# Attention products on GpSimd, and a seventh block in three passes for 12 more experts

## The chip, the cores and the metric

The kernel runs on one core of one Trainium2 chip. The core has five engines with a queue of instructions each: TensorE (PE in the profile, with its weight loads as PEld), VectorE (DVE), ScalarE (ACT), GpSimd (POOL) and SyncE (SP), which issues most of the DMAs. The engines run side by side and wait for each other through semaphores; each works through its own queue strictly in order. The metric is the device time of one execution in microseconds (us), lower being better.

## The reference

A block of sketched polynomial attention feeds a mixture of four experts. Cut to what is computed:

```python
# q, k, v: (4 batches, 4 heads, 1088 positions, 32); S1, S2: (8, 32)
def phi(x):
    a = einsum('rd,bhsd->bhsr', S1, x)
    b = einsum('rd,bhsd->bhsr', S2, x)
    return einsum('bhsi,bhsj->bhsij', a, b).reshape(..., 64)   # 64 products of factors
q_p, k_p = phi(q), phi(k)
kv = einsum('bhsf,bhsd->bhfd', k_p, v);  z = k_p.sum(axis=2)
x = (q_p @ kv) / (q_p @ z + 1e-6)          # -> (4352 tokens, 128)
p = domain_probs / (domain_probs.sum(-1) + 1e-9)
for e in range(4):                         # w1: (128, 1024), w2: (1024, 128) each
    out += p[:, e:e+1] * (maximum(x @ w1[e], 0) @ w2[e])
```

Everything is float32. The products in `phi` are what the change moves: for the keys 64 products per head and position (the "key products"), and the same for the queries (the "factor products").

## The kernel before

**Tiling.** The 4352 tokens are cut into 11 chunks (`CHUNKS`: 128, 448, 512, seven of 448, 128). A chunk goes through the four experts one after the other. An expert's 1024 hidden units are 8 blocks of 128, and a *half step* is one block of one expert for one chunk; a full chunk has 32 half steps and a step has two. `first` (from L1123) makes a block's hidden values: three matmuls of the kind fp32r, L1174, L1175 and (half a step later, in `third`) L1226, on weights and tokens that were split into parts called a, b and d. Between the second and the third ScalarE rescales the sum in PSUM (L1176). The first and the last chunk, of 128 tokens, go another way (`plain`), and so do the first two experts of chunk 1 (`whole`: three passes in the first matmul, plain fp32 in the second, L1276).

**The second matmul** of a block adds into the output, and there are two ways for it. In six of an expert's eight blocks (`THREE`) it is three fp32r matmuls (L1295, with `ha`, `hb`, `hd` as moving data): ScalarE makes `ha` (L1230), VectorE makes `hb` (L1202), and for two blocks at once `hd` (L1205). In the other two blocks ScalarE only takes the maximum with zero into `hid` (L1235) and the second matmul is one fp32 matmul, which the trace shows as two records. `MORE_IN` names the pairs (chunk, expert) in which seven blocks go through three passes and one stays fp32; `more_weight_parts` splits the weights of that seventh block (two activations on ScalarE, two operations on VectorE) at the steps in `MORE_AT`. `DEAL` and `DEAL_MORE` say how many half steps after a block's first matmul each of its second matmuls stands in TensorE's queue; the order is written out by hand and doesn't depend on when data is ready.

**After an expert**, `gather` (L1318) weights its output with the gate: ScalarE and VectorE bring the two PSUM banks together in `ev` (L1298, L1327), and GpSimd multiplies with the gate and adds to the chunk's `total` (L1334, L1336; two or four instructions). `ev` and `total` have one buffer each, `gate` has two, and SP's queue reloads a gate (L385) after GpSimd has read the one before it.

**Attention** is cut into three units per batch (`UNITS`), and its work is laid between the half steps by a plan (`lay_plan`): a list of pieces with a cost in VectorE time, each with an earliest place, so many half steps after another piece. `piece` takes the next piece when the credit that every half step brings suffices. For each unit: `qturn` (transposes on VectorE), `visit` of the unit before it (which projects this unit's queries on TensorE, copies them, L787, writes them to DRAM, L789, and reads them back spread over 128 partitions into `qp` and `qb`, L796 and L798), two `product` pieces (L810, at least `LAND` = 6 half steps after that visit), the unit's own `visit` on TensorE (`attend_products`: the factor products times the summed keys), `inverse`, `scale` and `out`. `out` transposes the unit's tokens and sends them over DRAM into `ring` (SP: four writes `xd<-y`, L744, then one read `ring<-xd`, L753), from where ScalarE and VectorE split them for the first matmul (`token_parts`, L925 and L928) at a fixed step, eight half steps ahead of their chunk. For each batch the keys go through `turn`, `project`, `sum` and four `products` pieces (L472, 576 elements per partition each); the sums over the keys (`key_sums`, 72 matmul records) stand in the visit of the last unit of the batch before, for batch 1 in a piece of its own.

What a visit's place is can be counted in TensorE's queue. Before, the projections of the visits stand behind the first matmul of half steps number 4, 15, 47, 65, 93, 107, 126, 157, 172 and 199, counted from the beginning of chunk 1, and the sums of the keys behind 38, 93 and 157.

Of the kernel before, what the change touches and what calls it, by code (L numbers as in the profile page):

```python
# [12 lines left out]
ALU = mybir.AluOpType  # L13
# [11 lines left out]
def kernel(  # L25
# [62 lines left out]
        ("b", 1, 1, 16), ("d", 1, 1, 17), ("b", 2, 0, 16), ("d", 2, 0, 17), ("b", 2, 1, 17), ("d", 2, 1, 18),  # L88
        ("a", 3, 1, 17), ("b", 3, 0, 19), ("b", 3, 1, 19), ("d", 3, 0, 20), ("d", 3, 1, 20),
    ]  # L90
    W2_AT = (36, 38), (41, 43), (45, 47), (65, 67)
    TOKENS_AT = 11, 12

    CHUNKS = [P, 448, 512] + [448] * 7 + [P]
    NC = len(CHUNKS)
    MORE_IN = {(7, 0), (7, 2), (8, 0), (8, 1), (8, 2), (9, 0), (9, 1), (9, 2), (9, 3)}
    MORE_AT = {0: (100, 102), 1: (113, 115), 2: (116, 118), 3: (129, 131)}
    START = [sum(CHUNKS[:m]) for m in range(NC)]
    assert all(sum(u) == S for u in UNITS) and sum(CHUNKS) == B * S

# [367 lines left out]
    def key_product(b, t0, n, p, x, eng, kf=None):  # L468

        if b:  # L470
            fs = lambda k, dims: _ap(fss[b], 0, P, 32 * (NT * p + t0) + R2 * x + k, [[32, n]] + dims)
            eng.tensor_tensor(  # L472
                out=_ap(kps[b], 0, P, 256 * t0 + P * p + R * x, [[256, n], [R2, R], [1, R]]),
                in0=fs(0, [[1, R], [0, R]]), in1=fs(R, [[0, R], [1, R]]), op=ALU.mult,
            )
            return
        src, off = (kf, P * p) if kf is not None else (fss[b], 32 * (NT * p + t0))
        eng.tensor_tensor(  # L478
            out=_ap(kps[b], 0, P, 256 * t0 + P * p + 64 * x, [[256, n], [32, 2], [R, 4], [1, R]]),
            in0=_ap(src, 0, P, off + 4 * x, [[32, n], [R2, 2], [1, 4], [0, R]]),  # L480
            in1=_ap(fss[b], 0, P, 32 * (NT * p + t0) + R, [[32, n], [R2, 2], [0, 4], [1, R]]),
            op=ALU.mult,
        )
# [44 lines left out]
    def key_pieces(b):  # L528

        for r in range(3):  # L530
            add(0.69 if r < 2 else 0.23, lambda r=r: key_turn(b, r), f"turn{r}")
        values, kf = value_copy(b), {}

        def project(gi):
            kf[gi] = held(psum(ps_h, "h"))
            key_project_wide(b, gi, kf[gi])

        def summed(gi):
            key_add(b, gi, kf[gi])
            free()  # L540
            next(values, None)
            if gi == 2 and 1 < b < B - 1:
                load_batch(b + 1)

        for gi in range(3):
            add(0.1, lambda gi=gi: project(gi), f"project{gi}", (f"turn{gi}", 2))
            add(0.2 if gi == 2 else 0.42, lambda gi=gi: summed(gi), f"sum{gi}", (f"project{gi}", 1))
        for p in range(2):
            for x in range(2):
                add(0.76, lambda p=p, x=x: key_product(b, 0, NT, p, x, nc.vector), "products")  # L550

    sums = {}

# [5 lines left out]
    def key_end(b):  # L559

        def blocked():
            key_blocks(b, sums.pop(b))
            free()

        if b == 1:
            add(0.1, lambda: key_sums(b), "keysum", ("products", 3))
        add(0.29, blocked, "keyblocks", ("keysum" if b == 1 else "visit", 1))

    def unit_parts(b, c, n):
# [237 lines left out]
    def unit_product(w, p):  # L807

        n, (qp, qb) = later[w][2], factors[w]
        nc.vector.tensor_tensor(out=qp[p][:, 0:n], in0=qp[p][:, 0:n], in1=qb[p][:, 0:n], op=ALU.mult)  # L810

    def unit_visit(w):

# [15 lines left out]
    def add(cost, run, name, after=None):  # L829

        plan.append((cost, run, name, after))

    def lay_plan():

        of_first = queries(0, P, UNITS[0][1])
        costs = [0.62] * 9 + [0.05] * 4 + [0.4, 0.55, 0.6, 0.1, 0.1]
        distances = {12: ("first8", 3), 13: ("first12", 1), 16: ("first15", 2), 17: ("first16", 2)}
        for at, cost in enumerate(costs):
            add(cost, lambda: next(of_first, None), f"first{at}", distances.get(at))
        covers.append((len(plan), P + UNITS[0][1]))  # L840
        add(vector_us(later[0][2]), lambda: unit_turn(0), "qturn", ("start", 2 * NQ - 2))
        add(0.1, lambda: unit_project(0), "visit", ("qturn", 6))
        add(0, lambda: None, "wait", ("start", 2 * NQ + 2))
        keys = {}
        for b in range(1, B):
            now_on, plan[:] = list(plan), []
            key_pieces(b)
            keys[b], plan[:] = list(plan), now_on
        for w, (b, c, n, u) in enumerate(later):
            if b == 0:  # L850
                plan.extend(keys[1][:9])
            else:
                at = {(1, 0): (1, 9, 13), (1, 1): (2, 0, 3), (1, 2): (2, 3, 5), (2, 1): (3, 0, 3), (2, 2): (3, 3, 9)}
                if (b, u) in at:
                    k, z0, z1 = at[b, u]
                    plan.extend(keys[k][z0:z1])
                if b == 1 and u == 0:
                    key_end(b)
            more = w + 1 < len(later)
            if more:  # L860
                add(vector_us(later[w + 1][2]), lambda w=w: unit_turn(w + 1), "qturn")
            for p in range(2):
                add(vector_us(n), lambda w=w, p=p: unit_product(w, p), "product", ("visit", LAND if w else LAND + 1))

            last = 0 < b < B - 1 and u == len(UNITS[b]) - 1
            if last:
                plan.extend(keys[b + 1][(5, 9)[b - 1] :])

            def visit(w=w, more=more, then=b + 1 if last else None):
                if then:  # L870
                    key_sums(then)
                if more:
                    unit_project(w + 1)
                unit_visit(w)

            add(0.1, visit, "visit", ("products" if last else "product", 3))
            if last:
                key_end(b + 1)
            add(0.4, lambda w=w: inverse.__setitem__(w, attend_inverse(*products[w])), "inverse", ("visit", 1))
            add(vector_us(n), lambda w=w: over.__setitem__(w, attend_scale(*products[w], inverse.pop(w))), "scale")  # L880
            add(vector_us(n), lambda w=w: unit_out(w), "out")
            covers.append((len(plan), S * b + c + n))
# [560 lines left out]
    def to_due(i):  # L1443

        m, kq = steps[i]
        e, f = divmod(kq, NP)
        if plain(m):
            due.append((2 * i + 5, 2 * i, 0, i, None, None))
        elif whole(m, e):
            late = (0, 0, 0, 0, 1, 1, 1, 1)[2 * f : 2 * f + 2] if e else (0, 0)  # L1450
            due.extend((2 * i + 3 + j + late[j], 2 * i, j, i, j, None) for j in range(2))
        elif f == 0:
            for at, (p, slot) in enumerate(deal_of(m, e).items()):
                k = int(p[1])
                due.append((2 * i + slot, 2 * i, at, i + k // 2, k % 2, p[0]))
        due.sort(key=lambda d: d[:3])
# [93 lines left out]
```

## Time and profile before

| what | value |
|---|---|
| time, median of 3 runs (lowest to highest) | 448.81 us (448.4 to 449.26) |
| the profiled execution: its time, its span | 448.88 us, 447.1 us |
| busy: PE, PEld, DVE | 442.2 us (99%), 370.7 us (83%), 371.4 us (83%) |
| busy: ACT, POOL | 333.8 us (75%), 128.4 us (29%) |
| granted clock of TensorE | 1.000 |
| DMA | 38.47 MB, mean 86 GB/s |
| DVE: L472 key products, 12 x 0.789 us | 9.5 us |
| DVE: L810 factor products, 20, by size 0.351 to 0.708 us | 11.8 us |
| POOL: L1334 and L1336, 126 instructions | 104.8 us |

The span is the time from the first to the last instruction of the profiled execution; the 1.8 us between it and the time lie around it. The busy time of PE counts the matmuls from the start of one to its modelled end, and one begins before the one before it has ended, so the distance from one start to the next is what a matmul costs when TensorE is the limit. The chain of waits goes back from the last instruction to whatever released each step. A line such as `L1176 ACT ... | 155.5, 540 | 74.9 <-PE h L1175 69.2` gives the busy time, the mean in ns of one, and the idle time of the engine before it with what ended it.

### The profile page before, as it was taken

What the parts mean: (1) busy time and instruction counts of PE and PEld (TensorE: products, weight loads), DVE (VectorE), ACT (ScalarE), POOL (GpSimd) and SP (SyncE); (2) the same over time, 40 slices, a digit from 0 to 9 for tenths busy, and PEclk for the clock granted to TensorE, in tenths of its full rate; (3) what the DMA queues carried; (4) which work ended last, traced back from release to release, by engine and by line L of the source; (5) the groups of instructions that cost most, each with busy time, mean ns of one, the idle gap of its engine ahead of it and who ended that gap; (6) DMA issues with size and microseconds to landing.
All of it is one profiled execution on the core that took longest, in us unless ns stands there. A gap on an engine that the chain in (4) does not pass through costs nothing.

```text
span 447.1 us, 8728 instructions
## 1 busy us (share of the span) xinstructions
PE 442.2 (99%) x3030; PEld 370.7 (83%) x3030; DVE 371.4 (83%) x634; ACT 333.8 (75%) x710; POOL 128.4 (29%) x211
## 2 busy tenths in 40 slices
PE   8999999999999999999999999999999999999997
PEld 5887678777788888888888888888888888888887
DVE  5998689897988896888879869898899898898853
ACT  4478878677867876778688767788788888888831
POOL 7346123211323141212321312124223313331430
PEclk9999999999999999999999999999999999999999
DMA  6956264014323402252242142410230021016401
GB/s 194 314 135 173 66 180 95 26 44 115 94 62 86 120 23 81 52 128 71 77 113 28 22 125 66 115 55 21 76 70 22 27 61 40 21 39 216 157 1 30
DMA packets 53620, 38.47 MB, mean 86 GB/s; under 512 B 26920, under 2 KB 49640, under 8 KB 53576
## 3 DMA queue, kind: packets, MB, share of 16 engines
q1 hardware_dynamic: 52776, 37.31, 31.2%
q0 software_dynamic: 576, 0.53, 0.6%
q8 instruction: 24, 0.39, 0.4%
q14 instruction: 20, 0.16, 0.1%
q10 hardware_dynamic: 224, 0.07, 0.1%
HBM read 32.68 MB, written 5.21 MB: 85 GB/s over the span
## 4 chain that ended last, share of the span: by engine, by line
PE 95%; DVE 2%; DMA 1%; issue 0%; SPq 0%; ACT 0%; DVEq 0%; ACTq 0%
PE o L1295 40%; PE h L1226 14%; PE h L1174 13%; PE h L1175 13%; PE h L261 7%; PE o L1276 3%; PE o L261 3%; PE h L456 1%; DMA kn<-in_k_dram 1%; DVE qp L609 1%; DMA vn<-in_v_dram 0%; DVE qa L900 0%; DVE rd L641 0%; DVE kp L478 0%; DVE qf L889 0%
## 5 line engine op out<-in xcount | busy, mean ns | idle before, releaser
L1176 ACT ACTIVATE h<-h 128x448 f32<-128x448 f32 (+1 forms) x288 | 155.5, 540 | 74.9 <-PE h L1175 69.2
L1202 DVE SCALAR_TENSOR_TENSOR hb<-h,ha 128x448 fp32r<-128x448 f32 (+1 forms) x213 | 130.3, 622 | 40.4 <-ACT ha L1230 37.7
L1205 DVE SCALAR_TENSOR_TENSOR hd<-ha,hb 128x896 fp32r<-128x896 f32 (+2 forms) x111 | 123.9, 1116 | 10.7 <-PE o L1295 1.9
L1174 PE MATMUL h<-xa,wa 128*128 128x448 f32 (+1 forms) x288 | 131.5, 457 | 0.0
L1230 ACT ACTIVATE ha<-h 128x448 fp32r<-128x448 f32 (+1 forms) x213 | 116.6, 547 | 0.0
L1334 POOL TENSOR_TENSOR ev<-ev,gate 128x256 f32<-128x256 f32 (+1 forms) x54 | 47.6, 881 | 214.5 <-DVE ev L1327 203.6
L1226 PE MATMUL h<-xd,wd 128*128 128x448 f32 (+1 forms) x288 | 107.3, 373 | 0.1
L1175 PE MATMUL h<-xb,wb 128*128 128x448 f32 (+1 forms) x288 | 105.8, 368 | 0.0
L1295 PE MATMUL o<-ha,vab 128*128 128x448 f32 (+1 forms) x204 | 76.4, 374 | 0.0
L1174 PEld LDWEIGHTS h<-xa,wa 128*128 128x128 f32 x288 | 54.2, 188 | 18.4 <-issue 13.5
L1175 PEld LDWEIGHTS h<-xb,wb 128*128 128x128 f32 x288 | 54.2, 188 | 17.8 <-issue 13.7
L1226 PEld LDWEIGHTS h<-xd,wd 128*128 128x128 f32 x288 | 54.0, 188 | 9.2 <-ACT h L1176 2.3
L1295 PE MATMUL o<-hd,vd 128*128 128x448 f32 (+1 forms) x204 | 60.1, 369 | 0.0
L1295 PE MATMUL o<-hid,w_sb 128*128 128x448 f32 (+1 forms) x118 | 54.7, 545 | 0.0
L1295 PE MATMUL o<-hb,vb 128*128 128x448 f32 (+1 forms) x136 | 50.1, 368 | 0.0
L1336 POOL TENSOR_TENSOR total<-total,ev 128x256 f32<-128x256 f32 (+1 forms) x54 | 45.0, 832 | 4.2
L1235 ACT ACTIVATE hid<-h 128x448 f32<-128x448 f32 (+1 forms) x75 | 41.5, 553 | 0.9 <-PE h L1226 0.8
L1295 PEld LDWEIGHTS o<-ha,vab 128*128 128x128 f32 x204 | 38.3, 188 | 4.2 <-issue 0.2
L1295 PEld LDWEIGHTS o<-hd,vd 128*128 128x128 f32 x204 | 38.1, 188 | 3.6
L1334 POOL TENSOR_TENSOR total<-ev,gate 128x256 f32<-128x256 f32 (+1 forms) x18 | 12.2, 699 | 71.7 <-issue 54.1
L1295 PEld LDWEIGHTS o<-hb,vb 128*128 128x128 f32 x136 | 25.5, 188 | 2.1
L1295 PE MATMUL o<-hb,vab 128*128 128x448 f32 (+1 forms) x68 | 25.3, 372 | 0.0
(151 smaller groups left out, 455.1 us busy)
## 6 DMA issues: line engine op xcount, KB each, us to landing
gate<-gates SPq DMA_DIRECT2D x22, 224.0 KB
kn<-in_k_dram SPq DMA_DIRECT2D x4, 544.0 KB
vn<-in_v_dram SPq DMA_DIRECT2D x16, 128.0 KB
w_last<-in_moe_w_dram SPq DMA_DIRECT2D x4, 512.0 KB
w_sb<-in_moe_w_dram SPq DMA_DIRECT2D x3, 512.0 KB
w_sb<-in_moe_w_dram SPq DMA_DIRECT2D x6, 256.0 KB
qp<-qd SPq DMA_DIRECT2D x6, 224.0 KB
qb<-qd SPq DMA_DIRECT2D x6, 224.0 KB
```

What stands on the lines that cost most here:

```text
L261: nc.tensor.matmul(out(s), weights(s), moving(s), **flags)
L1174: nc.tensor.matmul(g, wa[:, e, w], xa, start=True, stop=False)
L1175: nc.tensor.matmul(g, wb[:, e, w], xb, start=False, stop=True)
L1176: nc.scalar.activation(g, g, ACTF.Copy, scale=1.0 + R12)
L1202: nc.vector.scalar_tensor_tensor(out=hb, in0=g, scalar=0.0, in1=high, op0=ALU.max, op1=ALU.subtract)
L1205: nc.vector.scalar_tensor_tensor(out=d2, in0=a2.bitcast(F32), scalar=R12, in1=b2.bitcast(F32), op0=ALU.mult, op1=ALU.subtract)
L1226: nc.tensor.matmul(g, w, x, start=False, stop=True, skip_group_check=True)
L1230: nc.scalar.activation(ha, g, ACTF.Relu, scale=NEAR)
L1235: nc.scalar.activation(hid[i][j], g, ACTF.Relu)
L1295: nc.tensor.matmul(acc[m, e][o][:, 0:n], w, h, start=first_one, stop=last)
L1334: nc.gpsimd.tensor_tensor(out=to[:, x], in0=ev[:, x], in1=g[:, x], op=ALU.mult)
L1336: nc.gpsimd.tensor_tensor(out=total[m][:, x], in0=total[m][:, x], in1=ev[:, x], op=ALU.add)
```

## The change

Three things change together.

- The key products of `key_pieces` (L472) and the factor products of the later units (L810) are issued on GpSimd rather than on VectorE. In the plan their costs become smaller (0.4 and 0.3), they are kept apart from each other (two half steps between key products, one between factor products), and a visit comes at least 4 half steps after the second factor product, or 5 after the fourth key product, where it was 3.
- `MORE_IN` grows from 9 to 21 pairs: (1,2), (2,1), (3,0), (3,2), (4,0), (4,1), (5,0), (5,2), (6,0), (6,1), (7,1) and (8,3) are new. In each, one block's second matmul becomes three fp32r matmuls instead of one in fp32. The seventh block's weights, which were split in chunks 6 to 8, are split in chunks 1, 2 and 4 (`MORE_AT`).
- Two small moves in chunk 1: one piece of the weight splits comes half a step later (`W2_AT`), and one second matmul of its second expert half a step earlier (`late`).

```diff
-    W2_AT = (36, 38), (41, 43), (45, 47), (65, 67)
+    W2_AT = (36, 38), (41, 43), (45, 48), (65, 67)
...
-    MORE_IN = {(7, 0), (7, 2), (8, 0), (8, 1), (8, 2), (9, 0), (9, 1), (9, 2), (9, 3)}
-    MORE_AT = {0: (100, 102), 1: (113, 115), 2: (116, 118), 3: (129, 131)}
+    MORE_IN = {(1, 2), (2, 1), (3, 0), (3, 2), (4, 0), (4, 1), (5, 0), (5, 2), (6, 0), (6, 1), (7, 0), (7, 1), (7, 2)}
+    MORE_IN |= {(m, e) for m in (8, 9) for e in range(E)}
+    MORE_AT = {0: (37, 39), 1: (35, 36), 2: (22, 24), 3: (68, 70)}
...
-                add(0.76, lambda p=p, x=x: key_product(b, 0, NT, p, x, nc.vector), "products")
+                add(
+                    0.4,
+                    lambda p=p, x=x: key_product(b, 0, NT, p, x, nc.gpsimd),
+                    "products",
+                    ("products", 2) if p or x else ("sum2", 1),
+                )
...
-            add(0.1, lambda: key_sums(b), "keysum", ("products", 3))
+            add(0.1, lambda: key_sums(b), "keysum", ("products", 5))
...
-        nc.vector.tensor_tensor(out=qp[p][:, 0:n], in0=qp[p][:, 0:n], in1=qb[p][:, 0:n], op=ALU.mult)
+        nc.gpsimd.tensor_tensor(out=qp[p][:, 0:n], in0=qp[p][:, 0:n], in1=qb[p][:, 0:n], op=ALU.mult)
...
-                add(vector_us(n), lambda w=w, p=p: unit_product(w, p), "product", ("visit", LAND if w else LAND + 1))
+                add(
+                    0.3,
+                    lambda w=w, p=p: unit_product(w, p),
+                    "product",
+                    ("product", 1) if p else ("visit", LAND if w else LAND + 1),
+                )
...
-            add(0.1, visit, "visit", ("products" if last else "product", 3))
+            add(0.1, visit, "visit", ("products" if last else "product", 5 if last else 4))
...
-            late = (0, 0, 0, 0, 1, 1, 1, 1)[2 * f : 2 * f + 2] if e else (0, 0)
+            late = (0, 0, 0, 0, 0, 1, 1, 1)[2 * f : 2 * f + 2] if e else (0, 0)
```

After the change the projections stand behind half steps 4, 16, 47, 67, 97, 111, 132, 161, 175 and 200, and the sums of the keys behind 35, 97 and 161.

## Prediction

> **What bounds the kernel now.** I read the busy shares first, then the chain of waits, then the list of who waited for whom, and last TensorE's and SP's instructions in order of time. The page:
>
> ```profile
> PE 442.2 (99%) x3030; PEld 370.7 (83%) x3030; DVE 371.4 (83%) x634; ACT 333.8 (75%) x710; POOL 128.4 (29%) x211
> ...
> PE 95%; DVE 2%; DMA 1%; issue 0%; SPq 0%; ACT 0%; DVEq 0%; ACTq 0%
> ...
> L1205 DVE SCALAR_TENSOR_TENSOR hd<-ha,hb 128x896 fp32r<-128x896 f32 (+2 forms) x111 | 123.9, 1116 | 10.7 <-PE o L1295 1.9
> L1334 POOL TENSOR_TENSOR ev<-ev,gate 128x256 f32<-128x256 f32 (+1 forms) x54 | 47.6, 881 | 214.5 <-DVE ev L1327 203.6
> ```
>
> TensorE is the bound: 95% of the chain are matmuls. In the list of waits TensorE (PE, PEld) appears after the start only with small entries, the largest with a cause being the third pass behind ScalarE's rescaling, 2.3 us in all, 7 times. So work taken from VectorE gains nothing by itself; what counts is what TensorE executes, and whether something begins to be late for it. TensorE in order of time, in chunk 6:
>
> ```profile
> 288.16 0.36 PE L1174 MATMUL h<-xa,wa 128*128 128x448 f32 x1
> 288.36 0.37 PE L1175 MATMUL h<-xb,wb 128*128 128x448 f32 x1
> 288.56 0.36 PE L1226 MATMUL h<-xd,wd 128*128 128x448 f32 x1
> 288.76 0.56 PE L1295 MATMUL o<-hd,vd 128*128 128x448 f32 x2
> 289.17 0.91 PE L1295 MATMUL o<-hid,w_sb 128*128 128x448 f32 x2
> 289.57 0.71 PE L1174 MATMUL h<-xa,wa 128*128 128x448 f32 x1
> 290.12 0.36 PE L1175 MATMUL h<-xb,wb 128*128 128x448 f32 x1
> ```
>
> Starts of fp32r matmuls are 0.20 us apart. From the first record of the fp32 matmul (`hid`, 289.17) to L1175 (290.12) are 0.95 us with one L1174 in them: the fp32 matmul costs 0.95 - 0.20 = 0.75 us.
>
> **Part 1: 12 more experts with a seventh block in three passes.** Eleven fp32r matmuls from 397.93 to 400.16 give 0.203 us each, so three cost 0.61 and replace 0.75: 0.14 us saved per expert. The 512-column expert (2,1) saves 0.16 by the same reading of chunk 2. As a check, whole experts free of attention, from L1174 to L1174: (8,1), (8,2), (9,1), (9,2), which have the seventh block, take 9.89, 9.93, 9.89, 9.92; (4,0), (4,2), (6,0), (6,3), without it, 10.05, 10.04, 10.05, 10.04. That is 0.14 again. Gain: 11 x 0.14 + 0.16 = 1.7 us, all on the chain. The Trainium skill's page "FP8 and Floating Point Precision" (TensorE Precision Notes) counts four passes for true fp32. By four passes of 0.203 the gain would be 12 x 0.20 = 2.4 us and the time 446.9; the 0.75 measured here excludes it.
>
> On the other engines: ScalarE's L1235 (0.547 us) becomes L1230 (0.541), nothing. VectorE gets 12 x L1202 (0.615) and 12 x L1205 of 448 columns (0.626): +14.9 us. The weight splits only move (VectorE 0.326 + 0.268, ScalarE 2 x 0.312 per expert), into chunks 1, 2 and 4; in chunk 1 they take places that key products leave. The two small moves in chunk 1 shift one matmul and one split by half a step; I cost them at 0, between -0.3 and +0.3 (ScalarE's third-pass waits there are at most 0.4 us each).
>
> **Part 2: products on GpSimd.** VectorE loses 9.5 us (L472) and 11.8 (L810), so with part 1 its sum is 371.4 - 21.3 + 14.9 = 365.0 us. Laid out expert by expert with these means, no run of two or three experts asks more of VectorE than TensorE's time there: the worst single ones, (3,0), (4,0) and (6,0), ask 11.3 to 11.8 us, where TensorE needs 9.9 plus a visit of 1.4 to 3.8.
>
> GpSimd's own price: its gate product takes 0.59 us alone for 192 elements and 0.73 for 256, 0.0022 per element, so a factor product of 448 costs 1.15 and the 20 of them 19.9. Its key products at the start (L478: 0.625 for 256, 0.739 for 320) lead to 1.19 for 576, 12 of them 14.3. GpSimd goes from 128 to some 163 us, 36%; capacity is no issue. Two things may be: who meets whom, and when it is ready.
>
> Meeting: L1205 alongside a GpSimd tensor operation took 1.32 us in the mean (25 times), otherwise 1.06 (86 times); the longest 1.66. In the trace around a gate product at 62.68 to 64.48:
>
> ```profile
> 63.26 0.61 DVE L1202 SCALAR_TENSOR_TENSOR hb<-h,ha 128x448 fp32r<-128x448 f32 x1
> 63.91 1.52 DVE L1205 SCALAR_TENSOR_TENSOR hd<-ha,hb 128x896 fp32r<-128x896 f32 x1
> ```
>
> L1202, which reads PSUM, doesn't stretch; L1205, which reads SBUF twice, does, and L472 (0.75 alone, 1.21 there) too. With an L1205 every 3.2 us and products of 1.1, a third of 32 is met: 11 x 0.27 = 3 us more on VectorE, still below what it has now. Behind the stretched L1205 stand the next L1202 and TensorE's `hb` matmuls: from the end of L1202 to its matmul I count 2.1 us in the median, 0.4 at the least; for `hd` 2.2 and, but for the last expert, 0.7. A meeting costs TensorE only where it uses that up. With 108 GpSimd operations that meet L1205 already, TensorE doesn't wait. I take 0.15 us, between 0 and 3.0 (every met product reaching TensorE).
>
> Ready: the fourth key product stands behind the gather. In GpSimd's order, gather, three key products, gather, fourth key product: from one half step's first matmul to its gather take about 4 us, a gather 3.0 to 3.5, half steps 1.24. The second gather ends 9.9 + 4 + 3.3 = 17.2 us after the first one's half step, the fourth product 1.2 to 2 later at 18.4 to 19.2. The sums that read it begin at 18.2 with the other half of the products and need it at 19.3. Two visits (behind 97 and 161): 0.2 us, between 0 and 1.
>
> **Part 3: visits further behind.** This is the step with a price that a quick look would miss. The unit's tokens must be in `ring` when ScalarE splits them (L925), and that place doesn't move. Before, the ring's reads landed 1.36 us ahead of it (chunk 2), 3.91 (chunk 5) and 3.07 (chunk 7); elsewhere 2.8 and not moved, or over 5. L925 waits on ScalarE's queue in front of L1176, and the third pass starts 0.14 us after L1176 there: a late ring goes one for one to TensorE. The visit, whose reads the ring's writes follow through SP's queue, moves by 1, 4 and 3 half steps: measured on TensorE, the way from visit to L925 shrinks by 1.4, 5.4 and 3.2 us. That would leave 0, -1.5 and -0.1. But the visit also leaves a jam on SP:
>
> ```profile
> 187.06 1.93 SPq L1309 DMA_DIRECT2D out_dram<-ob  x4
> 189.03 1.14 SPq L789 DMA_DIRECT2D qd<-qs  x2
> ...
> 194.32 0.39 SPq L385 DMA_DIRECT2D gate<-gates  x1
> 195.07 1.80 SPq L744 DMA_DIRECT2D xd<-y  x4
> 201.52 0.33 SPq L753 DMA_DIRECT2D ring<-xd  x1
> ```
>
> `qs` was copied at 187.54 and its write issued only at 189.03 behind the output's writes; four half steps later these are gone: 1.4 us back in chunk 5, 1.5 in chunk 7. In the new order the gate's load stands ahead of `qd` and no longer ahead of `xd`, whose writes then follow the `qb` read (landed 199.64) by 0.75 rather than 1.7: 0.9 more. Margins: about 0 (chunk 2), +0.8 (chunk 5), +1 (chunk 7). I take 0.2 us for chunk 2 and nothing for the others; bounds 0 and 0.6 + 1.5 + 0.5 = 2.6.
>
> **Sum**, on the profiled execution of 448.88 us: -1.7 + 0 + 0.15 + 0.2 + 0.2 = -1.15, so 447.7; the median, 448.81, stands 0.07 lower: 447.6. Visits, transposes and copies keep their number, the end of the kernel is not touched.
>
> **Rivals.**
> - *The two engines hold each other up at SBUF* (slower). Products on GpSimd stretch L1205 as in the line above, `hb` and `hd` come late, and TensorE waits. For it: the stretch; against it: TensorE doesn't wait before, with the gather's 108 operations doing the same. If all 11 meetings cost TensorE their 0.27 us: -1.7 + 3.0 = +1.3, 450.1. It decides from 0.16 us per meeting on. The Trainium skill's page "SBUF — State Buffer" (SBUF: two separate sides) has a VectorE instruction with two SBUF inputs and a GpSimd one that reads SBUF exclude each other for a whole instruction. By that rule a met L1205 could wait a whole product; the trace agrees that it is L1205 that stretches, but by 0.6 us at the most.
> - *A late ring eats the gain* (no change). If the new SP order gives back nothing: -1.7 + 2.1 to 2.6, that is 449.2 to 449.7; if half: 448.4. For it: the exact margins in the trace; against it: the jam that disappears.
> - *Everything hides*: -1.7, 447.1. This belongs to the forecast's case.
>
> **How the numbers follow.** Forecast (gain of 1.0 to 1.8): 0.58, with its own range 446.9 to 447.9. Ring or key product eats about half or more, ending near 448.4: 0.24. Meetings on the chain or a full late ring, 449.2 to 450.1: 0.18. A measurement of this kernel tells 0.2% (0.9 us) from no change; the second case is mostly within it. So faster 0.59, within 0.2% 0.22, slower 0.19. Range: 446.9, the whole gain and the runs' spread, to 449.4; above it and below it 2 in 10 are left.
>
> **What would show it.** L1295 `o<-hid` falls from 118 to 94 records and the three-pass records rise by 36, TensorE's starts staying 0.20 apart; experts such as (4,2) keep 10.05 and (5,2) falls to 9.9 and what attention adds. L925 must show no wait on a DMA in chunks 2, 5 and 7; a wait there, with PEld L1226 waiting for ACT L1176, would be the second rival. PE waits of `o<-hb` or `o<-hd` on VectorE would be the first; a wait of the key sums on POOL L472 would show the fourth product late. I am wrong if VectorE is late for TensorE in the experts with both key products and a seventh block, or if TensorE has gaps that no row of before has.

## The result: 451.91 us, 0.7% slower

The changed kernel takes 451.91 us (median of 6 runs, 451.80 to 452.34), the kernel before 448.87 (6 runs, 448.40 to 449.26): a ratio of 1.0070, with a 95% interval of 1.0057 to 1.0083. The span grew from 447.1 to 450.2 us at a granted clock of 1.000 in both. The forecast of 447.6 is wrong in sign, and 451.91 lies above its range.

The page of the changed kernel (busy time, share of the span and instructions of each engine; share of the chain of waits; then groups with busy time, mean ns, and idle time before):

```profile
PE 443.0 (98%) x3042; PEld 373.0 (83%) x3042; DVE 384.0 (85%) x626; ACT 335.0 (74%) x710; POOL 172.4 (38%) x243
...
PE 29%; DVE 0%; issue 0%
...
L1216 DVE SCALAR_TENSOR_TENSOR hd<-ha,hb 128x896 fp32r<-128x896 f32 (+2 forms) x123 | 143.7, 1168 | 13.6 <-PE o L1306 3.9
...
L816 POOL TENSOR_TENSOR qp<-qp,qb 128x448 f32<-128x448 f32 (+5 forms) x20 | 25.5, 1289 | 5.0 <-DMA qb<-qd 5.0
```

TensorE is still the bound, and yet its busy time hardly changed (442.2 to 443.0): the time came as gaps. VectorE did not get lighter; it went from 371.4 to 384.0 us, where 365.0 were worked out. The chain breaks off after 29% here and tells no more. (Lines stand 1 to 11 further on than before: L472 is L473, L810 is L816, L1202 is L1213, L1205 is L1216, L1295 is L1306, L925 is L936, L753 is L759.)

The list of waits (total, times, longest, in us) has entries for TensorE that the kernel before doesn't have, all but the first of these:

```profile
PEld h L1237 <- ACT h L1187: 2.5, 7, 0.5
PEld o L1306 <- DVE hb L1213: 1.7, 4, 0.7
...
PEld h L262 <- POOL kp L473: 1.4, 2, 0.9
PEld o L1306 <- DVE ev L1338: 1.3, 3, 0.5
PE h L262 <- POOL kp L473: 1.1, 2, 0.8
...
PEld h L262 <- POOL qp L816: 0.6, 1, 0.6
```

To put sizes on them I took, for every pair of neighbouring matmul kinds, the median distance of their starts in the trace of before, and called what a distance exceeds it by a stall. A half step is named by its chunk, expert and number, or counted from the beginning of chunk 1, the first being 0; the places of visits and key sums are counted from 1, as in the kernel's description. By this reading the stalls grew by 4.9 us; with some 1.7 us saved by the seventh blocks that is about the 3.1 us lost. Each long stall is followed by a start 0.1 us later than usual (0.30 for 0.20 us); it is counted with it here, and what the same place takes in a kernel without the wait is taken off:

| where TensorE waits in the changed kernel | more than usual, us |
|---|---|
| sums of the keys, batches 2 and 3, for the fourth key product | 1.6 |
| visit behind half step 200, for the second factor product | 0.7 |
| `hb` in the third half step of (4,1) and of (6,1) | 1.0 |
| output bank (`ev` late on VectorE) in (1,3), (3,3), (5,3) | 0.9 |
| third pass behind ScalarE, half steps 18 and 43 | 0.5 |

The longest of them, at the sums of batch 3, in order of time (start, duration):

```profile
260.85 1.27 PE L262 MATMUL h<-vx,kp 128*64 128x66 f32 x36
262.89 0.92 PE L262 MATMUL h<-vx,kp 128*64 128x66 f32 x24 [0.77 <-POOL kp L473]
...
252.65 5.08 POOL L473 TENSOR_TENSOR kp<-fs 128x576 f32<-128x576 f32 x3
257.69 1.12 POOL L1345 TENSOR_TENSOR ev<-ev,gate 128x256 f32<-128x256 f32 x1
...
261.10 0.60 POOL L1347 TENSOR_TENSOR total<-total,ev 128x192 f32<-128x192 f32 x1
261.66 1.18 POOL L473 TENSOR_TENSOR kp<-fs 128x576 f32<-128x576 f32 x1
...
261.74 2.05 DVE L1216 SCALAR_TENSOR_TENSOR hd<-ha,hb 128x896 fp32r<-128x896 f32 x1
```

Three key products take 5.08 us where 3.6 were reckoned, the gather behind them is later for it, and the fourth product begins at 261.66, when TensorE has been in its sums for 0.8 us. It ends at 262.84; the second half of the sums starts at 262.89. VectorE's L1216, begun just behind the product, takes 2.05 us instead of 1.09 and ends 0.95 us after it.

SP in chunk 5, the place of the jam:

```profile
192.95 0.34 SPq L386 DMA_DIRECT2D gate<-gates  x1
194.12 1.32 SPq L795 DMA_DIRECT2D qd<-qs  x2
...
199.87 1.74 SPq L750 DMA_DIRECT2D xd<-y  x4
205.51 0.33 SPq L759 DMA_DIRECT2D ring<-xd  x1
```

The jam behind the output's writes is gone, and the gate's load stands ahead of `qd`, as foretold. The ring's read landed at 207.40 and ScalarE split it at 208.55, a margin of 1.15 us; in chunk 2 it is 0.38 us, in chunk 7 1.04. In no chunk does L936 wait for a DMA here.

### The profile page after: what moved, and what is told of

Its sections match the earlier page's. It is cut to its first block, busy times and chain, and to the rows that moved or that the text cites. A ratio compares the mean times of both kernels' runs of the same rounds, so it can differ in the third digit from the quotient of the medians.

```text
span 450.2 us, 8817 instructions
## 1 busy us (share of the span) xinstructions
PE 443.0 (98%) x3042; PEld 373.0 (83%) x3042; DVE 384.0 (85%) x626; ACT 335.0 (74%) x710; POOL 172.4 (38%) x243
## 5 line engine op out<-in xcount | busy, mean ns | idle before, releaser
L1213 DVE SCALAR_TENSOR_TENSOR hb<-h,ha 128x448 fp32r<-128x448 f32 (+1 forms) x225 | 136.4, 622 | 26.5 <-ACT ha L1241 21.9
L1216 DVE SCALAR_TENSOR_TENSOR hd<-ha,hb 128x896 fp32r<-128x896 f32 (+2 forms) x123 | 143.7, 1168 | 13.6 <-PE o L1306 3.9
L1185 PE MATMUL h<-xa,wa 128*128 128x448 f32 (+1 forms) x288 | 127.4, 442 | 0.0
L1241 ACT ACTIVATE ha<-h 128x448 fp32r<-128x448 f32 (+1 forms) x225 | 123.4, 548 | 0.7 <-PE h L1186 0.5
L1345 POOL TENSOR_TENSOR ev<-ev,gate 128x256 f32<-128x256 f32 (+1 forms) x54 | 50.6, 937 | 185.0 <-DVE ev L1338 175.3
L1306 PE MATMUL o<-ha,vab 128*128 128x448 f32 (+1 forms) x204 | 76.0, 373 | 0.0
L1306 PE MATMUL o<-hd,vd 128*128 128x448 f32 (+1 forms) x204 | 62.3, 371 | 0.0
L1306 PE MATMUL o<-hb,vb 128*128 128x448 f32 (+1 forms) x136 | 51.0, 375 | 0.5 <-DVE hb L1213 0.5
L1347 POOL TENSOR_TENSOR total<-total,ev 128x256 f32<-128x256 f32 (+1 forms) x54 | 43.6, 807 | 4.2
L1306 PE MATMUL o<-hid,w_sb 128*128 128x448 f32 (+1 forms) x94 | 44.0, 549 | 0.2
L1306 PEld LDWEIGHTS o<-ha,vab 128*128 128x128 f32 x204 | 38.3, 188 | 4.3 <-issue 0.2
L1306 PEld LDWEIGHTS o<-hd,vd 128*128 128x128 f32 x204 | 38.1, 188 | 3.6
L1246 ACT ACTIVATE hid<-h 128x448 f32<-128x448 f32 (+1 forms) x63 | 34.6, 550 | 0.9 <-PE h L1237 0.8
L1306 PEld LDWEIGHTS o<-hb,vb 128*128 128x128 f32 x136 | 25.6, 188 | 4.1 <-DVE hb L1213 1.7
L816 POOL TENSOR_TENSOR qp<-qp,qb 128x448 f32<-128x448 f32 (+5 forms) x20 | 25.5, 1289 | 5.0 <-DMA qb<-qd 5.0
```

The lines of the kernel that those rows point to most:

```text
L816: nc.gpsimd.tensor_tensor(out=qp[p][:, 0:n], in0=qp[p][:, 0:n], in1=qb[p][:, 0:n], op=ALU.mult)
L1185: nc.tensor.matmul(g, wa[:, e, w], xa, start=True, stop=False)
L1213: nc.vector.scalar_tensor_tensor(out=hb, in0=g, scalar=0.0, in1=high, op0=ALU.max, op1=ALU.subtract)
L1216: nc.vector.scalar_tensor_tensor(out=d2, in0=a2.bitcast(F32), scalar=R12, in1=b2.bitcast(F32), op0=ALU.mult, op1=ALU.subtract)
L1241: nc.scalar.activation(ha, g, ACTF.Relu, scale=NEAR)
L1246: nc.scalar.activation(hid[i][j], g, ACTF.Relu)
```

## The experiments

Each was timed in five rounds beside the kernel before on the same chip (448.77 to 448.96 there); ratios are to it, with the 95% interval. The first four take the change apart. Theory A: GpSimd is late with products. Theory B: the seventh blocks use up VectorE. Theory C: products on GpSimd stretch VectorE's L1216, and this reaches TensorE.

**Part 1 alone** (`seven_only`): `MORE_IN`, `MORE_AT`, `W2_AT` and `late` of the change in the kernel before.

> The kernel before with part 1 alone: the 12 more experts with a seventh block in three passes, their weight splits and the two small moves; all products stay on VectorE and the visits where they were. Theory A (TensorE waits for products that GpSimd finishes late; the seventh blocks are what they were priced at): 1.7 us faster than before, some 447.1 (446.8 to 447.6), no wait of TensorE for the hb line. Theory B (the seventh blocks themselves use up VectorE's time, so that hb and the output banks come late): the stalls of 0.36 and 0.46 us at experts (4,0) and (6,0), and those of 0.27, 0.26 and 0.15 us at the output banks stay, so 448.4 to 449.0. Theory C (VectorE is late only because L1216 is stretched by GpSimd's products): as A.

449.97 us, 1.0024 (1.0014 to 1.0033): theory B, and worse than it said, though at other places: `hb` isn't late at (4,1) and (6,1) here. The part that was to gain 1.7 us costs 1.0. Beside stalls at half steps 18, 24, 29, 43 and 64 the two largest are 0.56 and 0.50 us for `hb` in (3,3) and (5,3). In its trace (lines one further than before; the first rows are VectorE's, the last two TensorE's):

```profile
160.20 1.14 DVE L1203 SCALAR_TENSOR_TENSOR hb<-h,ha 128x448 fp32r<-128x448 f32 x2
161.45 1.09 DVE L1206 SCALAR_TENSOR_TENSOR hd<-ha,hb 128x896 fp32r<-128x896 f32 x1
162.45 0.76 DVE L473 TENSOR_TENSOR kp<-fs 128x576 f32<-128x576 f32 x1
163.12 0.62 DVE L1203 SCALAR_TENSOR_TENSOR hb<-h,ha 128x448 fp32r<-128x448 f32 x1
...
163.03 0.36 PE L1227 MATMUL h<-xd,wd 128*128 128x448 f32 x1
163.80 0.47 PE L1296 MATMUL o<-hb,vb 128*128 128x448 f32 x1 [0.40 <-DVE hb L1203]
```

VectorE has no gap over 0.11 us from 151.2 us on, near the beginning of (3,2); a key product stands ahead of the `hb` that TensorE wants next, and TensorE starts on it 0.06 us after it is there.

**Parts 2 and 3 alone** (`products_only`): the changed kernel with those four lines as before.

> The changed kernel with part 1 taken back: products on GpSimd with the visits further behind, but seventh blocks in 9 experts as before. Theory A: the waits for the fourth key product (0.51 and 0.96 us) and for the second factor product (0.61 us) stay, with some 0.1 us of restart each: 2.1 to 2.5 us slower than before, 451.0 to 451.4; the waits for hb are gone. Theory B (the seventh blocks are the cause of the rest): the same 451.0 to 451.4. Theory C (stretched VectorE instructions make TensorE wait by themselves): 1.5 us more of waits for hb and for output banks stay, 452.3 to 452.9.

450.71 us, 1.0040 (1.0026 to 1.0053). The waits for GpSimd stay (0.39 us in the sums of batch 2, 0.72 in batch 3, 0.65 in the visit), and one of 0.56 us in (1,3), for the ring of chunk 2, is new, told of below; none for `hb` or the output banks: theory A, 0.3 us less than it said; C alone is out. The parts add up: 1.04 + 1.78 = 2.82 of the 3.04 us. That is luck in part, for the waits are not the same ones: the changed kernel has no such stall for `hb` in (3,3) and (5,3) and none for the ring, and those at (4,1) and (6,1) are in neither part. With parts 2 and 3 in place, part 1 costs 1.2 us (450.71 to 451.91). On VectorE L1215 (`hd`) takes 131.1 us for the same 111 instructions that took 123.9, and the splits of tokens and weights, which read SBUF twice too, 5.1 us more; its busy time is 367.5, only 3.9 below before, though 21.3 us of products have left.

**Products back on VectorE, one kind at a time**, nothing else (`keys_back`, `factors_back`; TensorE's order is the changed kernel's to the instruction):

```diff
-lambda p=p, x=x: key_product(b, 0, NT, p, x, nc.gpsimd)
+lambda p=p, x=x: key_product(b, 0, NT, p, x, nc.vector)
```
```diff
-nc.gpsimd.tensor_tensor(out=qp[p][:, 0:n], in0=qp[p][:, 0:n], in1=qb[p][:, 0:n], op=ALU.mult)
+nc.vector.tensor_tensor(out=qp[p][:, 0:n], in0=qp[p][:, 0:n], in1=qb[p][:, 0:n], op=ALU.mult)
```

> The changed kernel with the key products alone back on VectorE, in the same places of the plan, so that TensorE's order is the same to the instruction. Theory A: the two waits of the key sums go (0.51 and 0.96 us and 0.1 each of restart), 1.7 us faster than the changed kernel, 450.2. Theory C: the waits for hb at experts (4,0) and (6,0) (0.36 and 0.46 us) go with them, since it is there that key products run beside L1216: 449.2 to 449.4. Theory B: VectorE gets 9.5 us more work in just the experts where it is late, so the hb waits grow: 450.2 to 451.9.

> The changed kernel with the factor products alone back on VectorE, in the same places. Theory A: the wait of the visit for the second factor product goes (0.61 us and some restart): 451.2; the two waits of the key sums stay. Theory C: the factor products are 20 of the 32, and the output banks that come late at chunks 2, 4 and 6 stand beside them; those stalls (0.68 us in all) go too: 450.4. Theory B: VectorE gets 11.8 us back, and is late more often: 451.2 to 452.5.

`keys_back`: 453.38 us, 1.0101 (1.0088 to 1.0115), beyond what any theory said. The waits of the key sums are gone, but the output banks wait 0.76, 0.61 and 0.60 us in (1,3), (3,3) and (5,3), and `hb` in five places: with seventh blocks beside them the key products cost VectorE more than GpSimd. The waits at (4,1) and (6,1) stay (0.35 and 0.45), so the key products are not their cause. `factors_back`: 451.10 us, 1.0051 (1.0039 to 1.0064). The visit's wait goes, as A says; that at (6,1) goes too and that at (4,1) falls from 0.36 to 0.18 us, as C says; new ones for `hb` in (5,3) (0.52 and 0.77 us) eat part of it. In the changed kernel, at (4,1):

```profile
184.84 1.28 DVE L1216 SCALAR_TENSOR_TENSOR hd<-ha,hb 128x896 fp32r<-128x896 f32 x1
186.04 0.69 DVE L602 STREAM_TRANSPOSE qT<-qn 128x256 f32<-128x256 f32 x2
186.67 0.58 DVE L1213 SCALAR_TENSOR_TENSOR hb<-h,ha 128x448 fp32r<-128x448 f32 x1
...
184.44 2.29 POOL L816 TENSOR_TENSOR qp<-qp,qb 128x256 f32<-128x256 f32 x2
...
186.73 0.37 PE L1237 MATMUL h<-xd,wd 128*128 128x448 f32 x1
187.30 0.47 PE L1306 MATMUL o<-hb,vb 128*128 128x448 f32 x1 [0.20 <-DVE hb L1213]
```

And with the factor products back on VectorE:

```profile
184.40 1.09 DVE L1216 SCALAR_TENSOR_TENSOR hd<-ha,hb 128x896 fp32r<-128x896 f32 x1
185.41 0.70 DVE L602 STREAM_TRANSPOSE qT<-qn 128x256 f32<-128x256 f32 x2
186.03 0.58 DVE L1213 SCALAR_TENSOR_TENSOR hb<-h,ha 128x448 fp32r<-128x448 f32 x1
...
186.28 0.37 PE L1237 MATMUL h<-xd,wd 128*128 128x448 f32 x1
186.67 0.47 PE L1306 MATMUL o<-hb,vb 128*128 128x448 f32 x1
```

From the third pass to the `hb` matmul it is 0.57 us with the two products beside L1216, and 0.39 without, where 0.20 is usual: the 0.19 that L1216 grew.

**Products ahead of the gather** (`ahead`, on `products_only`; `after_ahead`, the same edit on the changed kernel): the pieces keep their places in the plan, but the fourth key product goes out with the third, and the second factor product with the first.

```diff
-lambda p=p, x=x: key_product(b, 0, NT, p, x, nc.gpsimd),
+lambda p=p, x=x: [key_product(b, 0, NT, *at, nc.gpsimd) for at in ([(p, x)], [(1, 0), (1, 1)], [])[p + p * x]],
...
-lambda w=w, p=p: unit_product(w, p),
+lambda w=w, p=p: None if p else [unit_product(w, i) for i in range(2)],
```

> The kernel of products_only (450.71) with one thing changed on GpSimd's queue: the fourth key product is issued together with the third and the second factor product of a unit together with the first, so that neither stands behind a gather any more. TensorE's, VectorE's, ScalarE's and SP's orders stay. Theory A (TensorE waits for products that stand behind a gather on GpSimd): the waits of the key sums (0.39 and 0.72 us) and of the visit at half step 200 (0.65 us) go with their restarts; 1.5 to 2.3 us faster, 448.4 to 449.2. Rival (the price of GpSimd is the stretch of VectorE's L1216 and of the products themselves, wherever they stand; the gather, now 1.5 us later, holds up the output instead): no gain, 450.4 to 451.0.

448.70 us, 0.9998 (0.9989 to 1.0007): 2.0 us less than `products_only` by the order of GpSimd's queue alone, 1.7 of it behind half step 64, where the three waits were. In its trace the sums of batch 3 run through, all four products having ended before the gather:

```profile
259.23 2.31 PE L261 MATMUL h<-vx,kp 128*64 128x66 f32 x71
...
250.32 7.06 POOL L472 TENSOR_TENSOR kp<-fs 128x576 f32<-128x576 f32 x4
257.35 0.74 POOL L1344 TENSOR_TENSOR ev<-ev,gate 128x256 f32<-128x256 f32 x1
```

So theory A holds for parts 2 and 3, and without that fault they are worth nothing.

> The changed kernel with the one edit of the run ahead: the fourth key product beside the third and the second factor product beside the first, both before the gather. Theory (the stalls of the two parts add up): the key sums' waits (0.51 and 0.96 us) and the visit's (0.61 us) go with their restarts, 2.0 to 2.4 us: 449.5 to 449.9; the waits for hb at (4,1) and (6,1) and for the output banks stay. Rival (with seventh blocks beside them the gathers are late instead and the output banks wait more): 450.5 to 451.5.

450.73 us, 1.0034 (1.0021 to 1.0046): only 1.2 us less. The three waits are gone, but 1.13 us appear where the expectation hadn't looked: TensorE's third pass in (1,3) waits for ScalarE, and ScalarE's token split for the ring of chunk 2. That is the prediction's second rival; more below.

**Which seventh blocks cost** (on the kernel before, or on `seven_only`):

```diff
# pick: kernel before
-MORE_IN = {(7, 0), (7, 2), ...
+MORE_IN = {(3, 0), (4, 0), (4, 1), (5, 0), (6, 0), (6, 1), (7, 1), (8, 3), (7, 0), (7, 2), ...
-MORE_AT = {0: (100, 102), 1: (113, 115), ...
+MORE_AT = {0: (42, 44), 1: (52, 54), ...
# seven_late: seven_only without (1, 2), (2, 1)
# seven_apart: seven_only without (3, 2), (5, 2)
# splits_only: W2_AT, late and MORE_AT of the change, MORE_IN as before
```

> The kernel before with eight of the twelve new seventh blocks: (3,0), (4,0), (4,1), (5,0), (6,0), (6,1), (7,1), (8,3), which are the experts in which the run with part 1 alone showed no new stall; the weights of two experts are split earlier for it, in chunk 2 (first expert) and chunk 3 (second). Theory B (a seventh block gains its 0.14 us where VectorE has room and costs a stall where key products or weight splits stand beside it or just behind): 8 x 0.14 = 1.1 us faster than before, some 447.8 (447.5 to 448.3). Rival (the seventh block's load on VectorE shows up later wherever it is put): 448.7 to 449.5.

> Part 1 alone (449.97) without the new blocks of (1,2) and (2,1); the weights are split in chunks 1, 2 and 4 as in the change. The run with part 1 alone lost 0.6 us by the middle of chunk 2, where it should have gained 0.3. If the new blocks there are the cause: 449.1 to 449.4. If the weight splits moved into chunks 1 and 2 are: the same or 0.3 more, 449.9 to 450.3.

> Part 1 alone (449.97) without the new blocks of (3,2) and (5,2), the two experts ahead of those in which hb came 0.56 and 0.50 us late, while VectorE made the four key products. Theory B: the two waits go with 0.1 us of restart each, and 0.28 us of gain: 449.0 (448.8 to 449.2). Rival (the key products alone make hb late there, or the backlog comes from further ahead): 449.9 to 450.3.

> The kernel before with the weight splits in the places of the change (chunks 1, 2 and 4) and the two small moves, and no new seventh block. The run without the new blocks of (1,2) and (2,1) still lost 0.25 us at half step 18 and 0.30 at half step 43, where TensorE waits for ScalarE's rescaling, against the 0.3 expected at most: if the splits are the cause, 449.2 to 449.6, with these two waits; if the blocks of (3,x) and later pull something earlier, 448.9.

`pick`: 447.92 us, 0.9977 (0.9968 to 0.9986), 1.0 us below before, with no new stall: eight blocks give their eight times 0.14 where nothing stands in their way. It is faster than both kernels. `seven_late`: 449.21, 1.0005 (0.9997 to 1.0014), so the two blocks of chunks 1 and 2 cost 0.8 us rather than gain 0.3. `seven_apart`: 449.04, 1.0001 (0.9993 to 1.0010): (3,2) and (5,2) cost 0.9 and not gain 0.3, and the waits in (3,3) and (5,3) go with them. `splits_only`: 449.20, 1.0003 (0.9994 to 1.0012); by its times that is no difference, but the trace has the two waits of 0.15 and 0.19 us for ScalarE at half steps 18 and 43, and TensorE ends 0.26 us later. At half step 43 (ScalarE, then TensorE):

```profile
92.29 0.31 ACT L925 ACTIVATE vm<-w_sb 128x128 fp32r<-128x128 f32 x1 [0.61 <-DVE vm L928]
92.51 0.58 ACT L1176 ACTIVATE h<-h 128x512 f32<-128x512 f32 x1
...
92.72 0.40 PE L1175 MATMUL h<-xb,wb 128*128 128x512 f32 x1
93.14 0.50 PE L1226 MATMUL h<-xd,wd 128*128 128x512 f32 x1
```

The second split of a weight waits 0.61 us on VectorE's work on the first, and the rescaling that TensorE needs is queued behind it.

**Both parts together** (`pick_ahead`: `ahead` with the blocks and splits of `pick`; `ten_ahead`: also (3,2) and (5,2), with the third expert's split at 50 and 52 and the second's at 58 and 60).

> The run ahead (448.70) with the eight seventh blocks of the run pick. If the two add up: 448.70 - 1.0 = 447.7 (447.5 to 448.0). If the stretch of L1216 by products on GpSimd reaches TensorE once a seventh block has taken VectorE's reserve, which showed in the changed kernel at (4,1) and (6,1): 0.46 us each and no more than half of the gain, 448.3 to 448.9.

> The run before this one with (3,2) and (5,2) as well, and the third expert's weights split in chunk 3. With all key products on VectorE these two cost 0.6 us each, since hb was late at (3,3) and (5,3). If taking the products off VectorE makes room for them: 0.28 us faster than with eight, 447.4 or, with the waits at (4,1) and (6,1), 448.0 to 448.6. If not: 0.5 to 1.0 us slower than with eight.

`pick_ahead`: 449.88 us, 1.0021 (1.0012 to 1.0030). Two parts that are at or below the time before lose 1 us together. Its stalls: 0.41 and 0.49 us for `hb` at (4,1) and (6,1), as feared, and 0.95 us for the ring in chunk 2, as not. `ten_ahead`: 450.55, 1.0039 (1.0027 to 1.0052): taking the products off VectorE makes no room for (3,2) and (5,2); `hb` and the output bank of (3,3) wait 0.54 and 0.61 us.

**What the two waits need.** `ring_fix` is `ahead` with the first visit of chunk 1 back in its old place, `eight_ring` adds the blocks of `pick`, `six_ring` those without (4,0) and (6,0); `keys_eight` is `eight_ring` with all factor products on VectorE, one per piece again.

```diff
-add(0.1, visit, "visit", ("products" if last else "product", 5 if last else 4))
+add(0.1, visit, "visit", ("products" if last else "product", 5 if last else 4 if w else 3))
```

> The run ahead (448.70) with the first visit of chunk 1 three half steps behind its factor products rather than four, which is where it stood before the change. If the wait of the token split for the ring in chunk 2 (0.35 us at the third pass in ahead) comes from that half step: it goes, with 0.1 us of restart, 448.2 to 448.4. If the ring is late for another reason: 448.6 to 448.8, with the wait still there.

> The run ring_fix with six of the new seventh blocks: those of pick without (4,0) and (6,0). If hb at (4,1) and (6,1) is late only behind a seventh block: no wait of TensorE for hb, and 6 x 0.14 = 0.84 us faster than ring_fix, 447.3 to 447.6, less than either kernel. If the stretch of L1216 by the products on GpSimd reaches TensorE elsewhere: 448.2 or more.

> The run ring_fix with all eight blocks of pick, so pick_ahead (449.88) with the first visit back in its place. If the ring and the two late hb are what was lost there: the 0.95 us and its restart go, the two waits of 0.41 and 0.49 us stay, 448.6 to 449.0, that is 0.8 to 1.5 us above six_ring although it has two blocks more. If the ring was only where other time showed: 449.5 or more.

> The run eight_ring with the factor products back on VectorE; the key products stay on GpSimd. If it is the factor products' meeting with L1216 that makes hb late at (4,1) and (6,1): the two waits go with their restarts, 1.1 us faster than eight_ring, 447.4 to 447.9. If VectorE's load is what counts, whoever makes the products: 1.2 us more on VectorE per unit, hb later than in eight_ring, 448.8 to 449.8.

The `hb` side is nearly settled: `six_ring` (448.82, 1.0004, 0.9995 to 1.0012) has the products but not the blocks of (4,0) and (6,0), and no wait there; `keys_eight` (448.70, 0.9996, 0.9987 to 1.0005) has the blocks but not the factor products, no wait at (6,1), and 0.22 us left at (4,1); `eight_ring` (450.44, 1.0038, 1.0026 to 1.0051) has both, and 0.41 and 0.50 us. It takes both for the whole of it.

My guess on the ring was wrong: `ring_fix` takes 449.54 us (1.0017, 1.0008 to 1.0026), and its trace has a wait of 1.54 us. The two traces are single executions, that of `ahead` near its lowest time (448.45 of 448.27 to 449.69) and that of `ring_fix` near its highest (450.45 of 448.82 to 450.47), so that not all of the growth is the edit's; the medians are 0.8 us apart. `six_ring` and `eight_ring` missed their ranges with ring waits of 0.44 and 0.79 us, and `keys_eight`, which has no such wait, missed its own by 0.8 us all the same. How the ring gets late, the queues say in part. SP's gate load L385 waits until GpSimd has read the gate before it, in the gather, and the unit's writes `qd` stand behind that load. GpSimd, the load and the ring's read, and ScalarE's split in `ring_fix`:

```profile
47.48 1.68 POOL L815 TENSOR_TENSOR qp<-qp,qb 128x512 f32<-128x512 f32 x1 [6.24 <-DMA qb<-qd]
50.79 1.27 POOL L815 TENSOR_TENSOR qp<-qp,qb 128x512 f32<-128x512 f32 x1 [1.63 <-PE h L1185]
52.02 1.91 POOL L1344 TENSOR_TENSOR total<-ev,gate 128x256 f32<-128x256 f32 x2
...
53.96 0.34 SPq L385 DMA_DIRECT2D gate<-gates  x1
54.40 1.14 SPq L794 DMA_DIRECT2D qd<-qs  x2
...
66.73 0.34 SPq L758 DMA_DIRECT2D ring<-xd  x1
...
69.33 0.63 ACT L935 ACTIVATE xa<-ring 128x512 fp32r<-128x512 f32 x1 [1.49 <-DMA ring<-xd]
```

The same in the kernel before:

```profile
50.23 0.35 SPq L385 DMA_DIRECT2D gate<-gates  x1
51.97 1.14 SPq L789 DMA_DIRECT2D qd<-qs  x2
...
63.52 0.34 SPq L753 DMA_DIRECT2D ring<-xd  x1
```

GpSimd stands for 6.2 us before the first unit's read of `qb`, makes the first product, stands again for 1.6 us (put to a matmul here, to the read of `qb` in `pick_ahead` and `eight_ring`), makes the second, and only then the gather, which VectorE's `ev` had been ready for since 48.6. Over the kernels, in us, one execution each:

| | gather begins | gate's load | `qd` issued | ring's read issued | split waits for it |
|---|---|---|---|---|---|
| pick | 48.81 | 50.12 | 51.86 | 63.00 | - |
| before | 48.92 | 50.23 | 51.97 | 63.52 | - |
| factors_back | 49.25 | 50.56 | 53.65 | 64.88 | 0.05 |
| keys_eight | 49.30 | 50.60 | 52.34 | 63.77 | - |
| changed kernel | 49.80 | 51.67 | 53.93 | 65.06 | - |
| products_only | 49.99 | 51.84 | 53.90 | 64.86 | 0.5 |
| ahead | 50.61 | 52.56 | 53.57 | 64.67 | 0.3 |
| after_ahead | 51.99 | 53.93 | 54.37 | 65.84 | 1.1 |
| ring_fix | 52.02 | 53.96 | 54.40 | 66.73 | 1.5 |

In the last two rows `qd` follows the gate's load by 0.44 us: there the late gather holds it up. In four others, `factors_back`, the changed kernel, `products_only` and `ahead`, whose first visit stands one half step further behind than before, it comes 1.0 to 3.1 us behind the load. In `factors_back` the ring's read is 1.4 us late although gather and load are only 0.3 us later than before: that fits the place of the visit, the cause that the prediction had priced. Nor is the lateness handed on whole. In `ring_fix` the gather is 3.1 us later than before and the last `xd` write 1.8 us (61.84 for 60.07), but the ring's read is 3.2 us later; where the 1.4 us between write and read come from, no run shows.

**The first unit's products back on VectorE** (`unit0_back` on `ring_fix`, `six_unit0` on `six_ring`):

```diff
-nc.gpsimd.tensor_tensor(out=qp[p][:, 0:n], ...
+(nc.gpsimd if w else nc.vector).tensor_tensor(out=qp[p][:, 0:n], ...
```

> The run ring_fix (449.54, from 448.82 to 450.47) with the two factor products of the first unit back on VectorE; the other 18 factor products and the 12 key products stay on GpSimd, TensorE's, ScalarE's and SP's orders stay the same. If the ring was late because the products hold up the gather, and this the gate's load and SP's queue: the gate's load is back at 50 to 51 us, the wait of the token split goes, 448.6 to 448.9, and the spread over the runs falls to some 0.5 us. If the ring is late because of the visit's place or of DMA traffic: 449.0 or more with the wait still there.

> The same with six of the new seventh blocks, those of six_ring (448.82). By the same reading its wait of 0.44 us with 0.1 of restart goes: 447.9 to 448.3, about the time of pick, which has eight blocks and all products on VectorE. If GpSimd's products are worth something by themselves, below 447.7; if the wait stays, 448.6 to 449.0.

450.36 us (1.0034, 1.0023 to 1.0045; 449.10 to 451.60) and 449.33 (1.0011, 1.0001 to 1.0020): the expectation failed, with ring waits of 0.72 and 0.53 us, and the gate's load is at 52.69 and 52.60, not at 50 to 51. The edit moved the hold-up rather than took it away. Since both products go out in one piece, the second (49.51 on VectorE) now stands ahead of `ev`, which comes at 50.12 (48.22 in the kernel before, where the second product follows at 50.15), and the gather begins at 50.83. So the chain from a late gather to a late `qd` is seen in `after_ahead`, `ring_fix`, `six_ring`, `eight_ring` and these two, each with 0.44 to 0.46 us from the load to `qd`; that taking it away removes the wait is shown by `keys_eight` beside `eight_ring` alone, and a kernel with only this unit's products as before, one ahead of `ev` and one behind it, wasn't run.

## Why the prediction was wrong

- **Part 1, -1.7.** The price of a block was right: 0.14 us, eight of them 1.0 in `pick`, and (8,3), new among the 21, takes 9.9 us in the changed kernel, like (8,1) and (8,2). The step that failed is "no run of two or three experts asks more of VectorE than TensorE's time there". Sums over an expert don't see what stands ahead of one `hb`. In the kernel before, with the products still on VectorE, four of the twelve blocks, two in chunks 1 and 2 and two just ahead of experts with key products, cost 1.7 us and not gain 0.6, and the term measured +1.0 (`seven_only`). The changed kernel has the products off VectorE, as the step assumes, and it fails there too. From 178.1 us, in (4,0), to the late `hb` of (4,1) at 186.67 VectorE has no gap over 0.11 us; `hb` at (4,1) and (6,1) costs TensorE 1.0 us, late output banks 0.9, and the term is +1.2 (`products_only` to the changed kernel). The wait for the bank in (1,3) (0.23 us in `seven_only`) goes without the blocks of (1,2) and (2,1) in `seven_late`; what makes the other two banks late stays open.
- **Splits "only move", small moves 0.** 0.26 us in the trace of `splits_only`, whose times show no difference; within the bound of 0.3 given, and by the waits for ScalarE from which that bound was taken.
- **Meeting, 0.15.** The mechanism is right, its size on VectorE was not. In the changed kernel 42 of 90 L1216 with 896 columns meet a GpSimd tensor operation and take 1.41 us in the mean (longest 2.05) against 1.09 alone; before, 22 met one and took 1.31. The products stretch as well: the 12 of the keys 1.49 us each, not 1.19, those of the factors 25.5 us in all, not 19.9. Hence, with the splits of tokens and weights, which stretch too, 384.0 and not 365.0 us on VectorE. To TensorE it costs most of the 1.0 us at (4,1) and (6,1), and only behind a seventh block (0.18 us stay at (4,1) in `factors_back`). The Trainium skill's page "SBUF — State Buffer" (SBUF: two separate sides) lets such a VectorE and GpSimd instruction exclude each other, the one that begins first for its whole length. The trace agrees: each of the 37 L1216 with 896 columns that begin while a GpSimd tensor operation has at least 0.15 us to go ends 0.95 us after that operation's end, and `hb`, which reads PSUM, stays at 0.61 us. The kernel before shows the same in 18 of 18. So 0.27 us was what is left of gate products of 0.59 to 0.75 us, and not the price of a meeting: a product of 1.18 us cost up to 0.95. The prediction's "0.6 us at the most" compared the longest L1205, of 1024 columns, with the mean of all; and what the kernel before had shown to be harmless were the 25 meetings, not 108.
- **Ready, 0.2 (0 to 1).** The mechanism was named, the size was wrong by eight times: the key sums wait 1.6 us in the changed kernel, and all waits behind a gather together cost 1.7 of the 2.0 us between `products_only` and `ahead`. The gather's end was laid out with products of 1.19 us. The units' second factor products, which can stand behind a gather too, were not looked at: 0.7 us.
- **Late ring, 0.2.** No wait in the changed kernel, and the margins came out as foretold: 0.38 us in chunk 2 (about 0), 1.15 in chunk 5 (0.8), 1.04 in chunk 7 (1). Chunk 2 had nothing to spare and broke in `products_only` already. The step missed, which costs the changed kernel nothing, is that products on GpSimd can delay the gather, and with it the gate's load on SP.
- **The sum.** +1.0 and +1.8 give 2.8 of the 3.0 us, though not out of the same waits. The range ended at 449.4 because every case of the prediction, the slow ones too, counted the 1.7 us of part 1 as gained, and none had two rivals come true at once.

## What to carry to other kernels

An instruction moved to another engine's queue is priced by what stands ahead of it there and what it then stands ahead of: here a gather either way, once for 1.7 us on TensorE and once, over a gate's load and SP, for late writes of the queries. Work added to an engine that isn't the bound should be laid against the single instruction that the bound reads next, not against sums over a stage; eight places chosen so gain what twelve lose. Before two parts are joined, ask whether each gain lives off the same reserve; and when two parts measured alone add up to the whole, look whether they do so by the same waits.

## What the runs showed of the hardware

- Moving 21.3 us of two-input products from VectorE to GpSimd made them 43.9 us there (24.5 + 19.4 in `products_only`) and took 3.9 us off VectorE's busy time, since its other instructions with two SBUF inputs grew by some 12 us. A factor product of 448 columns takes 1.15 us when nothing holds it up and up to 2.15 beside VectorE's work, a key product 1.18 and up to 2.03.
- The time for which one of the two engines is shut out shows as a longer instruction, not as a gap: L1216 (896 columns, 1.09 us alone) ends 0.95 us after a GpSimd operation that began ahead of it (37 of 37), and a key product (1.18 alone) ends 1.04 to 1.05 us after an L1216 or its like that began ahead of it (2 of 2 in the changed kernel, 6 of 6 in `ahead`).
- After a wait TensorE's next start is 0.30 us away, not 0.20 (163.80 to 164.11 in `seven_only`), so that a stall costs 0.1 us more than the late start itself.
- With both products of the first unit in one piece ahead of the gather or of `ev` the run times spread: 448.82 to 450.47 in `ring_fix`, 449.10 to 451.60 in `unit0_back`, against 447.69 to 448.09 in `pick`. That the time of the unit's read from DRAM is what varies is likely and not shown.
